# Moving the additions to the output, the gathers of output rows and one unit of the expert order

## The chip, the cores and the metric

The kernel runs on one core of a Trainium2 chip. The metric is the device time of that core in microseconds (us) from launch to end; lower is better. TensorE does the matmuls and transpositions, VectorE (DVE in the profile) and ScalarE (ACT) the element work, GpSimd (POOL) issues the indirect DMAs here (gathers and scatters by a list of row numbers), and SyncE (SP) issues the plain loads.

## The reference, cut to what matters

The reference is pooled-query attention, then a gated feed-forward layer with RMS norm, then a layer of eight experts of which each token uses two. Only the last is touched by the change:

```python
logits = x @ w_gate
noisy_logits = logits + np.log1p(np.exp(x @ w_noise)) * noise
top2 = np.argpartition(-noisy_logits, 2, axis=1)[:, :2]
...                                   # softmax over the two
out = np.zeros((N, D))                # N = 1152 tokens, D = 512
for e in range(E):                    # 8 experts
    for k in range(2):
        mask = top2[:, k] == e
        h = np.maximum(x[mask] @ w1[e], 0.0)              # 512 -> 1024
        out[mask] += top2_w[mask, k, None] * (h @ w2[e])  # 1024 -> 512
```

## The kernel before, in words

The tokens of each expert are cut into blocks of up to 128. A *unit* is one expert with two blocks (a pair) or one block (a single); unit numbers go by the list `SEQ`. Units 0 and 1 are pairs that are chosen early. Before the change units 2, 4, 6, 8, 10, 11 and 13 are pairs and units 3, 5, 7, 9 and 12 are singles. A further set of units behind a branch is for uneven routings; it does not run with these inputs.

Each unit has eight steps, `i` = 0 to 7. Steps 0 to 3 multiply the tokens by a quarter of `w1` each (`up_pair`, `up_one`; tile `ph`), steps 4 to 7 multiply the hidden values by a quarter of `w2` each and accumulate in PSUM (`down`; tile `py`). Every float32 product is made from rounded high and low parts with three passes: high by high, the low part of the tokens, the low part of the weights. ScalarE rounds the high part, and VectorE subtracts it to get the low part. The pieces around a unit are:

- `wsplit` (lines 106 and 1006): splits one quarter of weights, `raw`, into `wz`. It runs five steps ahead of its use (`LEAD = 5`), one at the end of each step, and it sets off the load of the same quarter two units later (SP, line 961).
- `gather_x` (L1022): gathers the token rows `xg`, with their weights, for the unit two ahead; one buffer.
- `x_trans` (L973, L976, L978): in step 5 TensorE transposes the next unit's tokens into a PSUM bank, ScalarE writes the high part and VectorE the low part of `xgT`. `weight` (L1120, L1122; tile `wv`) follows.
- `h_trans` (the same lines, tile `hTT`): singles alone transpose their hidden values, one half after step 2 and the other after step 4. `bank()` gives these transpositions and those of `x_trans` two PSUM banks in turn, so the second block's `x_trans` in a single takes the bank of the second `h_trans`.
- `gather_o` (L1028): gathers the rows of `out` that the unit will add to, tile `pr`, one buffer.
- `finish` (L1133, L1134): VectorE computes `yo = py * weight + pr`, and POOL scatters `yo` to `out`; for a pair there are two additions and two scatters. It is called for unit u-1 while unit u runs.

All instructions stand in the program order in which Python calls these functions, and each engine takes its own in that order. Every scatter to `out` and every gather from it waits for the scatter before it to land, since all touch the same DRAM tensor. So there is a loop through memory: the additions of a unit lead to its scatters, these to the gather of output rows of the next unit, and this to that unit's additions.

Of the kernel before, what the change touches and what calls it, by code (L numbers as in the profile page):

```python
# [21 lines left out]
def fused_kernel(ctx, tc, q, k, v, w_gate, w_val, w_out, rms_g,  # L22
# [895 lines left out]
    def r_index(pl):  # L918
# [12 lines left out]
    RAW = []  # L931
    REG = {}
    SEQ = [None, None] + [(True, 0), (False, 0), (True, 1), (False, 1), (True, 2), (False, 2), (True, 3), (False, 3),
                          (True, 4), (True, 5), (False, 4), (True, 6)]
    NU1 = len(SEQ)
    SEQ += [(True, r) for r in range(NPS, NPA)] + [(False, r) for r in range(NSS, NSA)]

    def nblk(u):
        return 2 if u < 2 or SEQ[u][0] else 1
# [48 lines left out]
    def experts():  # L988
# [5 lines left out]
        def wload(u, i):  # L994
            if i == 0:
                c = ucol(u, 0) if u > 1 else 1
                REG[u] = sp.value_load(R["ti" if u > 1 else "ea"][0:1, c:c + 1], min_val=0, max_val=NE - 1)
            e_dma(u, i)
# [9 lines left out]
        def wsplit(u, i):  # L1008
            w_hi(u, i)
            w_lo(u, i)  # L1010

        def col(u, k, nm):
            if u < 2:
                return R[nm + "0"][:, 2 * u + k:2 * u + k + 1]
            c = ucol(u, k)
            return R[nm][:, c:c + 1]

        def gather_x(u):
            XG[u] = mo.tile([P, 2, XW], F32, name="xg", tag="xg", bufs=1)
            for k in range(nblk(u)):  # L1020
                gi = col(u, k, "gidx")
                pool.indirect_dma_start(out=XG[u][:, k], out_offset=None, in_=XD if u > 1 else XD[0:QF],  # L1022
                                        in_offset=bass.IndirectOffsetOnAxis(ap=gi, axis=0))

        def gather_o(u):
            PR[u] = wps[0].tile([P, 2, DM], F32, name="pr", tag="ws21", bufs=1)
            for k in range(nblk(u)):
                pool.indirect_dma_start(out=PR[u][:, k], out_offset=None, in_=out,  # L1028
                                        in_offset=bass.IndirectOffsetOnAxis(ap=col(u, k, "gidx"), axis=0))
# [28 lines left out]
        def x_trans(u):  # L1058
            run(x_trans_(u))

        def h_trans(u, h):
            run(h_trans_(u, h))
# [30 lines left out]
        def down(u, i, k):  # L1093
            if (u, "y", k) not in PL:
                PL[u, "y", k] = pbank("py")
            w, x = W[u, i], HTT[u]
            f0 = 2 * (i - 4)
            for z, (a, c) in enumerate(PASS):
                for d in range(2):
                    pe.matmul(PL[u, "y", k], x[c][:, f0 + d, k * P:k * P + P], w[a][:, d],  # L1100
                              start=i == 4 and z + d == 0, stop=i == 7 and z == 2 and d == 1)

        def piece(u, i):
            if i >= 4:
                for k in range(nblk(u)):
                    down(u, i, k)
            elif nblk(u) == 2:
                up_pair(u, i, 0)
                up_pair(u, i, 1)
                up_evac(u, i)  # L1110
            else:
                up_one(u, i)

        def weight(u):
            n = nblk(u)
            xg = XG[u]
            wv = WV[u] = mo.tile([P, 3, 2], F32, name="wv", tag="wv", bufs=3)
            e = R["eb"][:, ucol(u, 0):ucol(u, 0) + 1] if u > 1 else R["ef"][:, u:u + 1]
            for z in range(2):
                dve.scalar_tensor_tensor(wv[:, z, 0:n], xg[:, 0:n, DM + 2 + z], e, xg[:, 0:n, DM + z],  # L1120
                                         op0=ALU.is_equal, op1=ALU.mult)
            dve.tensor_tensor(wv[:, 2, 0:n], wv[:, 0, 0:n], wv[:, 1, 0:n], op=ALU.add)  # L1122

        def finish(u, ks=None):
            if u not in YO:
                YO[u] = mo.tile([P, 2, DM], F32, name="yo", tag="yo", bufs=1)
            yo = YO[u]
            for k in range(nblk(u)) if ks is None else ks:
                w = WV[u][:, 2, k:k + 1]
                if u == 0:  # L1130
                    dve.tensor_scalar(yo[:, k], PL[u, "y", k], w, 1.0, op0=ALU.mult, op1=ALU.mult)
                else:
                    dve.scalar_tensor_tensor(yo[:, k], PL[u, "y", k], w, PR[u][:, k], op0=ALU.mult, op1=ALU.add)  # L1133
                pool.indirect_dma_start(out=out, out_offset=bass.IndirectOffsetOnAxis(ap=col(u, k, "sidx"), axis=0),  # L1134
                                        in_=yo[:, k], in_offset=None, bounds_check=B * SQ - 1, oob_is_err=False)
# [7 lines left out]
        def units(u0, u1, skip=0):  # L1143
            todo = [(u, i) for u in range(u0, u1) for i in range(8)]
            if not skip:
                gather_x(u0)
                gather_o(u0)
                for i in range(8):
                    wload(u0, i)
                for a in todo[:LEAD]:  # L1150
                    wsplit(*a)
                x_trans(u0)
                weight(u0)
                if u0 + 1 < u1:
                    gather_x(u0 + 1)
                    for i in range(8):
                        wload(u0 + 1, i)
                for u, i in todo[:LEAD]:
                    if u + 2 < u1:
                        wload(u + 2, i)  # L1160
            for n_, (u, i) in enumerate(todo):
                if n_ < skip:
                    continue
                last = u == u1 - 1
                if not last or i < 4:
                    piece(u, i)
                if nblk(u) == 1:
                    if i == 2:
                        h_trans(u, 0)
                    if i == 4 - last:  # L1170
                        h_trans(u, 1)
                if u > max(u0, 1):
                    if i == (1 if last else 3):
                        finish(u - 1)
                    if i == (1 if last else 6):
                        gather_o(u)
                if i == 5 and u + 1 < u1:
                    x_trans(u + 1)
                    weight(u + 1)
                    if u + 2 < u1:  # L1180
                        gather_x(u + 2)
                if n_ + LEAD < len(todo):
                    v_, j = todo[n_ + LEAD]
                    wsplit(v_, j)
                    if v_ + 2 < u1:
                        wload(v_ + 2, j)

            u = u1 - 1
            for k in range(nblk(u)):
                for i in range(4, 8):  # L1190
                    down(u, i, k)
                finish(u, [k])
# [4 lines left out]
        def rest():  # L1197
            open_psum()
            PL[1, "y", 0] = pbank("py")
            units(0, NU1, 8)  # L1200
            more = nc.values_load(R["more"][0:1, 0:1], min_val=0, max_val=1)  # L1201
            with tc.If(more > 0):
                units(NU1, len(SEQ))
# [53 lines left out]
    for f in range(2, NFP - 2):  # L1257
        u0 = 32 * f
        for s_, a in zip(T_E, ((f, 2), (f + 1, 0), (f + 1, 1))):
            dec(u0 + s_, *a)  # L1260
    u0 = 32 * (NFP - 2)
# [204 lines left out]
```

## Time and profile before

| what | value |
|---|---|
| median of 3 runs | 841.33 us (839.68 to 841.87) |
| the profiled execution, its own time | 845.55 us |
| span of that execution, first to last instruction | 843.3 us |
| TensorE busy | 794.3 us (94%) |
| VectorE busy | 581.2 us (69%) |
| ScalarE busy | 422.0 us (50%) |
| GpSimd busy | 303.6 us (36%) |
| mean granted TensorE clock | 0.976 of full speed |

The profiled execution took 4.2 us more than the median of the runs. TensorE's share is high everywhere; what a change in the last stage is worth has to be read from that stage, which runs from about 568 us to the end.

### The profile page before, as it was taken

Reading aid. Unit: us, or ns where it says so; the run is one execution under the profiler, and the core shown is the slowest. Engines: PE = TensorE matmul, PEld = TensorE weight load, DVE = VectorE, ACT = ScalarE, POOL = GpSimd, SP = SyncE. Lnnn points to the kernel's source line nnn. Section 1 sums busy time; section 2 is a strip of 40 time slices with the busy share of each in tenths; the row PEclk is TensorE's granted clock in tenths of the full one; section 3 lists DMA queues with packets and bytes.
Section 4 is the critical chain, followed back from the end, with each engine's and each line's share of the span. In section 5 each row is a group of like instructions: output and inputs, shape, how many; then the busy total and the mean of one; then the engine's idle time right before and its main releaser. Section 6 shows DMA issues by size and latency. Waiting matters only on the chain. (4 is left out here: it accounts for less than half of the span.)

```text
span 843.3 us, 14029 instructions
## 1 busy us (share of the span) xinstructions
PE 794.3 (94%) x5282; PEld 683.7 (81%) x5282; DVE 581.2 (69%) x838; ACT 422.0 (50%) x823; POOL 303.6 (36%) x251
## 2 busy tenths in 40 slices
PE   5999999999897979999999999999999899989994
PEld 4877777777675779998999999879989798889883
DVE  6668668677679866665687646597676677676680
ACT  4655655656665644442343252555455556554550
POOL 8647647649224531312132100113133332422331
PEclk9999999999999989999999999999999999999997
DMA  7245232221132211422142016649987879787411
GB/s 215 72 136 154 54 98 75 58 84 30 43 115 59 92 51 51 130 79 92 51 141 63 1 51 218 203 148 373 314 286 243 291 254 312 256 289 233 140 44 39
DMA packets 72939, 118.83 MB, mean 141 GB/s; under 512 B 7582, under 2 KB 37278, under 8 KB 72864
## 3 DMA queue, kind: packets, MB, share of 16 engines
q1 hardware_dynamic: 67504, 101.55, 37.8%
q0 software_dynamic: 5360, 16.31, 5.5%
q8 instruction: 43, 0.70, 0.4%
q14 instruction: 32, 0.26, 0.1%
HBM read 103.66 MB, written 10.77 MB: 136 GB/s over the span
## 5 line engine op out<-in xcount | busy, mean ns | idle before, releaser
L528 PE MATMUL gv<-XN,ws 128*128 128x256 f32 (+1 forms) x1152 | 168.1, 299 | 4.4 <-ACT sl L536 4.0
L528 PEld LDWEIGHTS gv<-XN,ws 128*128 128x128 f32 x1152 | 159.8, 191 | 10.3 <-ACT sl L536 4.2
L1006 DVE TENSOR_TENSOR wz<-raw,wz 128x1024 fp32r<-128x1024 f32 x112 | 133.8, 1222 | 22.9 <-ACT wz L106 22.3
L193 DVE TENSOR_REDUCE Ql<-s 128x1 fp32r<-128x1152 f32 x72 | 97.3, 1354 | 58.7 <-PE s L188 44.7
L1100 PE MATMUL py<-wz,hTT 128*128 128x512 f32 x552 | 137.2, 401 | 0.0
L204 ACT ACTIVATE et<-st 128x288 f32<-128x288 f32 x288 | 103.0, 413 | 52.8 <-PE st L203 48.5
L1100 PEld LDWEIGHTS py<-wz,hTT 128*128 128x128 f32 x552 | 102.9, 192 | 20.9 <-DVE hTT L978 0.7
L106 ACT CAST wz<-raw 128x1024 fp32r<-128x1024 f32 x112 | 113.4, 1046 | 8.0 <-PE py L1100 8.0
L398 POOL TENSOR_TENSOR ws<-wm,ws 128x1024 fp32r<-128x1024 f32 x18 | 43.3, 2407 | 150.7 <-ACT ws L397 96.4
L202 PE MATMUL st<-QH,KT 128*128 128x288 f32 x288 | 91.3, 332 | 5.3 <-ACT et L204 3.8
L1073 PEld LDWEIGHTS ph<-xgT,wz 128*128 128x128 f32 x768 | 92.8, 189 | 0.7
L1073 PE MATMUL ph<-xgT,wz 128*128 128x256 f32 x768 | 92.8, 281 | 0.0
L549 PE MATMUL po<-ws,hT 128*128 128x512 f32 x324 | 84.6, 400 | 0.1
L203 PE MATMUL st<-QlT,KT 128*128 128x288 f32 x288 | 82.2, 299 | 0.0
L229 PE MATMUL av<-et,v 128*64 128x288 f32 x576 | 81.9, 420 | 0.0
L1134 POOL DMA_INDIRECT out_dram<-yo,sidx x23 | 32.1, 1395 | 131.5 <-DVE yo L1133 96.0
L202 PEld LDWEIGHTS st<-QH,KT 128*128 128x128 f32 x288 | 55.0, 191 | 20.6 <-ACT et L204 11.5
L217 POOL TENSOR_TENSOR accp<-accp,et 128x576 f32<-128x576 f32 x32 | 48.6, 1519 | 55.8 <-ACT et L204 35.1
L549 PEld LDWEIGHTS po<-ws,hT 128*128 128x128 f32 x324 | 59.5, 192 | 11.1 <-ACT hT L538 0.5
L538 ACT CAST hT<-sl 128x256 fp32r<-128x256 f32 (+1 forms) x48 | 20.8, 433 | 89.8 <-DVE sl L537 89.8
L229 PEld LDWEIGHTS av<-et,v 128*64 128x64 f32 x576 | 37.6, 138 | 26.0 <-issue 5.9
L203 PEld LDWEIGHTS st<-QlT,KT 128*128 128x128 f32 x288 | 55.5, 193 | 0.0
(250 smaller groups left out, 1142.6 us busy)
## 6 DMA issues: line engine op xcount, KB each, us to landing
raw<-in_moe_w_dram SPq DMA_DIRECT2D x112, 512.0 KB, 4.6
wraw<-in_moe_w_gate_dram SPq DMA_DIRECT2D x6, 1024.0 KB, 5.5
wraw<-in_moe_w_val_dram SPq DMA_DIRECT2D x6, 1024.0 KB, 6.7
wraw<-in_moe_w_out_dram SPq DMA_DIRECT2D x6, 1024.0 KB, 5.1
kraw<-in_k_dram SPq DMA_DIRECT2D x16, 288.0 KB, 3.8
v<-in_v_dram SPq DMA_DIRECT2D x8, 576.0 KB, 3.7
KT<-KT SPq DMA_DIRECT2D x16, 288.0 KB, 3.3
Qraw<-in_q_dram SPq DMA_DIRECT2D x16, 256.0 KB, 3.9
```

Of the source, the lines that this page charges most:

```text
L106: act.copy(o, i)
L193: dve.tensor_reduce(Ql[p % 3][h][:, c, D:D + 1], t[:, :, 0:384], axis=AX.XY, op=ALU.max, negate=True)
L202: pe.matmul(t[:, 0:NG], KT[p, h][:, cs], QhT[p, h][:, n0:n0 + NG], start=True, stop=False)
L203: pe.matmul(t[:, 0:NG], KT2[h][p % NKT[h]][:, cs], QlT[p, h][:, n0:n0 + NG], start=False, stop=True)
L204: act.activation(et[:, h, :], t[:, 0:NG], AF.Exp, scale=SCALE)
L217: eng.tensor_tensor(acc, acc, e, op=ALU.add)
L229: pe.matmul(av[h * D:(h + 1) * D, 0:NG], V[p][:, h, c, :], ET[p, g, c][:, h, :], start=(c == 0), stop=(c == KC - 1))
L528: pe.matmul(t[:, 0:n], w[a][:, d, j * P:(j + 1) * P], XN[hf][b_][:, d, cs], start=(k_ == 0), stop=(k_ == 11))
L549: pe.matmul(pt, HT[f, hf][a][:, j, c0:c0 + P], w[b_][:, j, :], start=(k_ == 0), stop=(k_ == 5))
L1006: eng.tensor_tensor(lo, RAW[u % 2][i], hi.bitcast(F32), op=ALU.subtract)
L1073: pe.matmul(o, w[a][:, d, j * P:j * P + P], XT[u][c][:, d], start=z + d == 0, stop=z == 2 and d == 3)
L1100: pe.matmul(PL[u, "y", k], x[c][:, f0 + d, k * P:k * P + P], w[a][:, d], start=i == 4 and z + d == 0, stop=i == 7 and z == 2 and d == 1)
```

## The change

It does three things. `finish(u - 1)` is called in a pair at step 4 instead of step 3, and in a single at step 5 instead of step 3; the call now stands behind `x_trans`, `weight` and `gather_x` of the same step. `gather_o(u)` is called in a pair at step 5 instead of step 6, and in a single at step 7 instead of step 6. The last unit keeps step 1 for both. And the fifth single changes places with the sixth pair behind it in the list: units 10 to 13 are now pair, single, pair, pair.

```diff
     SEQ = [None, None] + [(True, 0), (False, 0), (True, 1), (False, 1), (True, 2), (False, 2), (True, 3), (False, 3),
-                          (True, 4), (True, 5), (False, 4), (True, 6)]
+                          (True, 4), (False, 4), (True, 5), (True, 6)]
...
-                if u > max(u0, 1):
-                    if i == (1 if last else 3):
-                        finish(u - 1)
-                    if i == (1 if last else 6):
-                        gather_o(u)
                 if i == 5 and u + 1 < u1:
                     x_trans(u + 1)
                     weight(u + 1)
                     if u + 2 < u1:
                         gather_x(u + 2)
+
+                f_, g_ = (1, 1) if last else (4, 5) if nblk(u) == 2 else (5, 7)
+                if u > max(u0, 1):
+                    if i == f_:
+                        finish(u - 1)
+                    if i == g_:
+                        gather_o(u)
                 if n_ + LEAD < len(todo):
```

On VectorE the first place is a single, from the low part of its first hidden half to the first weights behind the next unit's tokens. Before:

```order
L978 TENSOR_TENSOR hTT<-xt,hTT 128x4x128
L1006 TENSOR_TENSOR wz<-raw_5871,wz 128x1024
L1133 SCALAR_TENSOR_TENSOR yo<-py,wv,pr 128x512 x2
L1006 TENSOR_TENSOR wz<-raw_5581,wz 128x1024
L978 TENSOR_TENSOR hTT<-xt,hTT 128x4x128
L1006 TENSOR_TENSOR wz<-raw_5581,wz 128x1024
L978 TENSOR_TENSOR xgT<-xt,xgT 128x4x128 x2
L1120 SCALAR_TENSOR_TENSOR wv<-xg,eb 128x2 x2
L1122 TENSOR_TENSOR wv<-wv 128x2
L1006 TENSOR_TENSOR wz<-raw_5582,wz 128x1024 x2
```

With the change the same stretch of a single on VectorE reads:

```order
L978 TENSOR_TENSOR hTT<-xt,hTT 128x4x128
L1006 TENSOR_TENSOR wz<-raw_5871,wz 128x1024
L1006 TENSOR_TENSOR wz<-raw_5581,wz 128x1024
L978 TENSOR_TENSOR hTT<-xt,hTT 128x4x128
L1006 TENSOR_TENSOR wz<-raw_5581,wz 128x1024
L978 TENSOR_TENSOR xgT<-xt,xgT 128x4x128 x2
L1120 SCALAR_TENSOR_TENSOR wv<-xg,eb 128x2 x2
L1122 TENSOR_TENSOR wv<-wv 128x2
L1133 SCALAR_TENSOR_TENSOR yo<-py,wv,pr 128x512 x2
L1006 TENSOR_TENSOR wz<-raw_5582,wz 128x1024 x2
```

The two additions `yo` of the pair before have moved from ahead of the second `hTT` to behind the next unit's `xgT` and `wv`.

The second place is POOL's queue over a single and the pair behind it, from the gather of token rows or the scatters of the single's steps to the pair's gather of output rows. Before:

```order
L1134 DMA out_dram<-yo,sidx 1152x512 x2
L1022 DMA xg<-XD,gidx 128x516
L1028 DMA pr<-out_dram,gidx 128x512
L1134 DMA out_dram<-yo,sidx 1152x512
L1022 DMA xg<-XD,gidx 128x516 x2
L1028 DMA pr<-out_dram,gidx 128x512 x2
```

With the change POOL takes the same stretch in this order:

```order
L1022 DMA xg<-XD,gidx 128x516
L1134 DMA out_dram<-yo,sidx 1152x512 x2
L1028 DMA pr<-out_dram,gidx 128x512
L1134 DMA out_dram<-yo,sidx 1152x512
L1022 DMA xg<-XD,gidx 128x516 x2
L1028 DMA pr<-out_dram,gidx 128x512 x2
```

In the single the gather of token rows now stands ahead of the two scatters; the order within the pair is the same, although its calls stand at other steps.

## Rows read from the trace of the kernel before

**Rows 1.** Waits in the expert stage: waiter <- releaser: us in total, times, longest.

```profile
PE xt L973 <- DVE hTT L978: 10.5, 5, 3.6
```

**Rows 2.** Timeline of unit 5, second half: start, duration, work [idle before <-releaser].

```profile
662.35 0.75 DVE L1133 SCALAR_TENSOR_TENSOR yo<-py,wv,pr 128x512 f32<-128x512 f32 x1 [2.21 <-DMA pr<-out_dram,gidx]
...
665.99 0.69 PE L973 MATMUL xt<-ident,xg 128*128 128x128 f32 x4 [3.59 <-DVE hTT L978]
666.40 4.58 PE L1100 MATMUL py<-wz,hTT 128*128 128x512 f32 x12
...
670.82 11.56 PE L1073 MATMUL ph<-xgT,wz 128*128 128x256 f32 x96
```

**Rows 3.** Timeline around the end of unit 12, TensorE and VectorE.

```profile
805.43 0.66 PE L973 MATMUL xt<-ident,xg 128*128 128x128 f32 x4 [0.85 <-DVE hTT L978]
805.84 3.00 PE L1100 MATMUL py<-wz,hTT 128*128 128x512 f32 x12
...
808.00 0.16 DVE L1122 TENSOR_TENSOR wv<-wv 128x2 f32<-128x2 f32 x1
808.68 11.69 PE L1073 MATMUL ph<-xgT,wz 128*128 128x256 f32 x96
```

**Rows 4.** Stretches of 20 us: PE, PEld, DVE, ACT, POOL busy, granted clock, DMA share, GB/s.

```profile
640.00:660.00 20.00, 20.00 (x122) 17.61 (x121) 13.42 (x16) 11.14 (x14) 7.80 (x6) 1.00 0.71 235
660.00:680.00 20.00, 16.41 (x109) 14.93 (x108) 13.40 (x18) 9.36 (x13) 4.92 (x4) 0.91 0.89 297
```

**Rows 5.** Timeline from unit 3's scatters through unit 4 into unit 5.

```profile
624.68 2.00 POOL L1134 DMA_INDIRECT out_dram<-yo,sidx  x1 [5.94 <-DVE yo L1133]
...
629.71 11.56 PE L1073 MATMUL ph<-xgT,wz 128*128 128x256 f32 x96
...
632.87 1.00 POOL L1134 DMA_INDIRECT out_dram<-yo,sidx  x1 [6.18 <-DVE wz L1006]
...
639.82 0.96 POOL L1028 DMA_INDIRECT pr<-out_dram,gidx  x1 [4.66 <-DMA out_dram<-yo,sidx]
...
646.25 0.75 DVE L1133 SCALAR_TENSOR_TENSOR yo<-py,wv,pr 128x512 f32<-128x512 f32 x1 [3.62 <-DMA pr<-out_dram,gidx]
...
652.48 4.39 PE L1088 MATMUL ph<-wz,xgT 128*128 128x256 f32 x36
...
657.07 1.22 DVE L1006 TENSOR_TENSOR wz<-raw,wz 128x1024 fp32r<-128x1024 f32 x1 [2.20 <-ACT wz L106]
```

**Rows 6.** Timeline: first scatters in units 5 and 7, additions in units 6 and 8.

```profile
664.28 1.96 POOL L1134 DMA_INDIRECT out_dram<-yo,sidx  x1 [7.22 <-DVE yo L1133]
...
683.66 0.74 DVE L1133 SCALAR_TENSOR_TENSOR yo<-py,wv,pr 128x512 f32<-128x512 f32 x1
...
703.47 1.97 POOL L1134 DMA_INDIRECT out_dram<-yo,sidx  x1 [5.75 <-DVE yo L1133]
...
723.52 0.75 DVE L1133 SCALAR_TENSOR_TENSOR yo<-py,wv,pr 128x512 f32<-128x512 f32 x1 [2.15 <-DMA pr<-out_dram,gidx]
```

**Rows 7.** Timeline of POOL in units 12 and 13.

```profile
803.26 1.02 POOL L1134 DMA_INDIRECT out_dram<-yo,sidx  x1 [4.58 <-DVE yo L1133]
...
806.84 1.00 POOL L1134 DMA_INDIRECT out_dram<-yo,sidx  x1 [2.56 <-DVE wz L1006]
...
809.90 1.75 POOL L1028 DMA_INDIRECT pr<-out_dram,gidx  x1 [2.06 <-DMA out_dram<-yo,sidx]
```

**Rows 8.** The tile `pr`, its gathers, all of the execution.

```profile
DMA to landing us min/median/max: 4.7/5.8/9.2
```

**Rows 9.** Timeline of unit 13: the additions on VectorE and the last scatter.

```profile
815.88 0.74 DVE L1133 SCALAR_TENSOR_TENSOR yo<-py,wv,pr 128x512 f32<-128x512 f32 x1
...
825.88 0.75 DVE L1133 SCALAR_TENSOR_TENSOR yo<-py,wv,pr 128x512 f32<-128x512 f32 x1 [4.16 <-PE py L1100]
...
832.35 1.00 POOL L1134 DMA_INDIRECT out_dram<-yo,sidx  x1 [4.42 <-DVE yo L1133]
```

**Rows 10.** Waits of VectorE in the expert stage, as in rows 1.

```profile
DVE yo L1133 <- DMA pr<-out_dram,gidx: 11.4, 9, 3.6
```

## The prediction

> **What bounds the kernel now.** I read the waits of the expert stage first, then the timeline of the singles, then the gathers and scatters. TensorE is busy nearly without a break in the pairs; its one wait of size stands in the five singles. There it has the transposition of the second token block to do, and the bank for it is freed by VectorE's low part of the second hidden half: 10.5 us in five waits [rows 1]. The timeline of unit 5 shows why VectorE is late. Two additions stand ahead of that low part, and the first waits 2.21 us for its gathered output rows; TensorE starts at 665.99, after 3.59 us idle [rows 2]. In unit 12 the output rows are there in time, the additions cost their two times 0.75 us, and the wait is 0.85 us [rows 3].
>
> The idle time has a second price. After it the twelve matmuls of the next two steps took 4.58 us in unit 5 [rows 2] against 3.00 in unit 12 [rows 3], and the granted clock of that stretch is 0.91 where the one before had 1.00 [rows 4]. Unit 9 repeats this; the other three singles, with shorter waits, do not.
>
> Behind this stands a loop through memory. The single scatters its pair's sums, one scatter after the other, then the single's own output rows are gathered, and the next pair adds to them. From the first scatter to that addition it took 646.25 - 624.68 = 21.6 us [rows 5] and 723.52 - 703.47 = 20.1 [rows 6], where the addition was waiting. At the other two it was not waiting, so that the chain took at most 683.66 - 664.28 = 19.4 [rows 6]; I use 19.0.
>
> **The change, part by part.**
>
> *The wait of TensorE goes.* In a single the additions now stand behind the low parts and the weights of the next tokens. Ahead of the second hidden half only splits are left, which ScalarE feeds. In unit 12 the two additions are 1.5 us of work for a wait of 0.85 [rows 3], so taking them out leaves nothing there; in the other four the wait for output rows leaves too. This removes 10.5 us [rows 1], and the slow matmuls twice, 2 x (4.58 - 3.00) = 3.2 [rows 2, 3]. I leave 0.1 per single, 0.5 in all (bounds: 0, and unit 12's 0.85 each, 4.3), for the last split to finish. Net gain 13.2 us.
>
> *The addition in the pair becomes later than VectorE wants it.* Call the pair's first matmul p. In unit 12 the weights of the next tokens were done at 808.16, 0.5 us before p = 808.68 [rows 3]. TensorE's bank and VectorE's later instructions both follow from the second hidden half, so this distance should hold. POOL then issues the gather of token rows of that step, which now stands ahead of the scatters; with an issue of 1.0 us, as those of the scatters [rows 7], and a start on either side of it, an estimate of 0.5 each, the first scatter follows at about p + 1.5. It can't be before p + 0.3, when the first sum is ready, and two issues of 2.0 us as that of 624.68 [rows 5] would make it p + 2.5. Before, it was 5.0 us ahead of p in unit 3 (624.68 against 629.71 [rows 5]) and 6.5 in unit 5 [rows 2, 6]. The chain then ends at p + 23.1, 20.5, 21.6 and 20.5 for the four pairs behind a single with weights still being loaded. VectorE comes to the addition at 683.66 - 670.82 = 12.8 after p [rows 2, 6] and, one step later, behind one split more of 1.2, at p + 14.1. So it will stand for 6 to 9 us at each of these, against 3.6 in unit 4.
>
> What is queued behind it: one split, the low part of the single's tokens, its weights, and the splits for the single. ScalarE and TensorE go on, since the pair's own weights were split five steps ahead. In unit 4 VectorE came out of its wait at 646.25 - 629.71 = p + 16.5, and in the single behind it still had 2.20 us of idle time at 657.07, just ahead of the first hidden half that TensorE waits for [rows 5]. The change leaves one split (1.2) less between. So TensorE loses nothing up to p + 16.5 + 2.2 + 1.2 = p + 19.9, and from there on microsecond for microsecond. The loss is 3.2 + 0.6 + 1.7 + 0.6 = 6.1 us. It is cut into two waits, at the single's start and at its hidden half, so that it is less likely to bring the clock down: I take half of one 1.6 us, 0.8 (bounds 0 and 3.2).
>
> The bounds of this term: nothing if all four chains are like the short ones and the scatter starts at p + 0.3 (19.7), and 4 x 3.2 = 12.8 if all are like that of unit 3.
>
> A rule of the Trainium skill bears on the hops of the chain ("DMA: Bandwidth & Descriptors", section "Anatomy of one DMA — SWDGE (gpsimd) path"): about 2.0 us fixed plus the bytes over 436 GB/s. For a block of 262 KB it would give 2.6 us a hop, and with three issues of 1 us a chain of about 11 us and no new wait at all. While weights are loaded this case's hops took 8.2 and 6.9 us from scatter to scatter and from scatter to gather [rows 5]; without loads 3.6 and 3.1 [rows 7], which is near the page. The sum goes by the rows.
>
> *The pair's gather of output rows one step earlier* is hidden: POOL takes it behind the two gathers of token rows as before, and these wait for VectorE's weights, so an earlier call is worth nothing. The single's gather one step later waits for the second scatter anyway; it too changes nothing. The gather of token rows that now goes ahead is not needed before the next unit's step 5.
>
> *The order of units.* The number of units and matmuls stays. The weights of the last unit are loaded by the third step of unit 11, which is now the single, so the chain that starts there runs without loads: 3.6 + 3.1 [rows 7] + at least 4.7 [rows 8], with p + 1.5 it ends near p + 13, before VectorE asks. No wait there. But the last unit now finishes a pair: two scatters, the second behind the first. Its additions ran 815.88 - 808.68 = 7.2 after its start [rows 3, 9]; 1.0 to the scatter, 3.6 to the second, 3.1 to the gather of output rows, 5.0 until they are added: 19.9, against 825.88 - 808.68 = 17.2 when TensorE had the first block ready [rows 9]. The first of the last two scatters comes at 20.9, the second 3.6 behind at 24.5, against 832.35 - 808.68 = 23.7 [rows 9]. That is 0.8 later, 1.9 if the gather lands in its median 5.8 [rows 8]. I take 1.0.
>
> **The sum.** -13.2 + 6.1 + 0.8 + 1.0 = -5.3 us. The profiled execution's own 845.55 becomes 840.2; it stands 4.2 above the median of the runs, 841.33, which becomes 836.0. A measurement of this kernel can tell about 0.3% from no change, 2.5 us: faster is below 838.8, slower above 843.9.
>
> **Rivals.**
>
> *The chain is hidden (0.17).* If the hops are shorter while VectorE stands still and sets off no weight loads, the chain ends by p + 19.9 everywhere. For it: two of four were at most 19.4. Against it: the other two. Time: -13.2 + 1.0 = -12.2, 829.1. The skill's rule on the hops, above, would end here.
>
> *The gain is eaten (0.17).* The loop through memory sets the pace of a pair and a single, wherever the additions stand. For it: unit 3's chain of 21.6, and VectorE waiting for output rows already, 11.4 us in all [rows 10]. If all four chains took that long: -13.2 + 12.8 + 0.8 + 1.0 = +1.4, 842.7.
>
> *Slower: the wait at the pair's addition grows (0.12).* Place: the addition in the pair's step 4. A gather of output rows took up to 9.2 us to land [rows 8], against 6.4 in unit 3's chain (639.82 to 646.25 [rows 5]). Two such chains of 24.4 end at p + 25.9 and cost 6.0 each; two of 21.6 cost 3.2 each; TensorE then waits long enough in one piece for the slow matmuls twice: 18.4 + 3.2 + 1.0 - 13.2 = +9.4, 850.7. It decides from a mean end of the chain of about p + 23.5, where four losses of 3.6 plus 0.8 and 1.0 exceed the gain by 2.5.
>
> **How the numbers follow.** My forecast has 0.54: a gain of 2.6 to 11 us, most likely 5.3. With the hidden chain that makes faster 0.71; same 0.17; slower 0.12. The range reaches from the hidden chain, 829, to the eaten gain with one more microsecond, 843.5; I leave about 0.2 outside, more of it above.
>
> **What would show it right or wrong.** The wait of TensorE for the second hidden half should fall from 10.5 us to under 1, and the matmuls behind it should take 2.9 to 3.0 us. VectorE's wait for output rows should rise from 11.4 [rows 10] to between 25 and 35 us, nearly all in four additions at 20 to 23 us after their pair's start. TensorE should show new waits for `xgT` or the first `hTT` in the singles behind them, 6 us in all. The last scatter should start about 24.5 us after the last unit. It is wrong if the pair's additions wait little (time near 829), or if token rows, whose gather stands behind VectorE's wait in the pair, reach the next single's step 5 too late. I cost that at nothing: behind the addition VectorE has one split, one low part and the weights, some 3 us, before these gathers can go, and the single's second transposition could start 665.99 - 3.59 - 652.48 = 9.9 us into it [rows 2, 5], about 12 after the addition; a landing later than that costs TensorE as much as it is late, four times.

## The result and the profile after

The changed kernel took 833.14 us in the median of its runs against 841.33 before: a ratio of 0.9902, with a 95% interval of 0.9877 to 0.9927, 8.2 us faster. That lies inside the range, and the forecast of 836.0 named the right side, but the gain is half as large again as the 5.3 us that were forecast. The profiled execution took 833.25 us (span 831.1), which is near its median; that of before, at 845.55, stood 4.2 above its own. So the two profiles differ by 12.3 us and the medians by 8.2, and what follows counts in the profiles first.

The waits of the expert stage after the change (waiter <- releaser: us in total, times, longest); the last is all that TensorE's matmuls wait for in the stage:

```profile
DVE yo L1133 <- DMA pr<-out_dram,gidx: 26.1, 7, 5.8
...
PE xt L973 <- DMA xg<-XD,gidx: 0.5, 1, 0.5
```

TensorE's 10.5 us behind `hTT` [rows 1] are gone. The other row is the time that VectorE stands idle for output rows (its *stand*, below), which rose from 11.4 us [rows 10] to 26.1: the wait was not removed, it was moved to VectorE, as the prediction said. Of the 26.1 us 18.8 lie in the four pairs that the prediction meant, 4.3 to 5.4 each, and 5.8 in the last unit.

Unit 5, the pair behind it and the last two units in the timeline (start, duration, work, in brackets the idle time before and what ended it):

```profile
658.35 1.08 PE L973 MATMUL xt<-ident,xg 128*128 128x128 f32 x8
...
659.19 3.02 PE L1100 MATMUL py<-wz,hTT 128*128 128x512 f32 x12
...
661.54 1.41 DVE L1133 SCALAR_TENSOR_TENSOR yo<-py,wv,pr 128x512 f32<-128x512 f32 x2
662.05 11.56 PE L1073 MATMUL ph<-xgT,wz 128*128 128x256 f32 x96
663.44 1.53 POOL L1134 DMA_INDIRECT out_dram<-yo,sidx  x1 [0.30 <-issue]
...
670.93 1.00 POOL L1134 DMA_INDIRECT out_dram<-yo,sidx  x1 [5.96 <-DVE wz L1006]
...
676.72 0.99 POOL L1028 DMA_INDIRECT pr<-out_dram,gidx  x1 [4.80 <-DMA out_dram<-yo,sidx]
...
681.80 0.75 DVE L1133 SCALAR_TENSOR_TENSOR yo<-py,wv,pr 128x512 f32<-128x512 f32 x1 [5.37 <-DMA pr<-out_dram,gidx]
...
684.82 4.39 PE L1088 MATMUL ph<-wz,xgT 128*128 128x256 f32 x36
...
793.56 11.69 PE L1073 MATMUL ph<-xgT,wz 128*128 128x256 f32 x96
...
800.76 1.40 DVE L1133 SCALAR_TENSOR_TENSOR yo<-py,wv,pr 128x512 f32<-128x512 f32 x2
801.78 1.02 POOL L1134 DMA_INDIRECT out_dram<-yo,sidx  x1 [7.32 <-DVE yo L1133]
...
810.19 0.96 POOL L1028 DMA_INDIRECT pr<-out_dram,gidx  x1 [0.30 <-issue]
...
812.45 0.75 DVE L1133 SCALAR_TENSOR_TENSOR yo<-py,wv,pr 128x512 f32<-128x512 f32 x1 [5.84 <-DMA pr<-out_dram,gidx]
...
815.00 1.02 POOL L1134 DMA_INDIRECT out_dram<-yo,sidx  x1 [3.85 <-DMA pr<-out_dram,gidx]
...
816.21 0.75 DVE L1133 SCALAR_TENSOR_TENSOR yo<-py,wv,pr 128x512 f32<-128x512 f32 x1 [3.01 <-PE py L1100]
820.37 1.00 POOL L1134 DMA_INDIRECT out_dram<-yo,sidx  x1 [4.34 <-DMA out_dram<-yo,sidx]
```

*The single* (the first three kinds of row). The transpositions of both token blocks now run as one group of eight without a wait at 658.35, the twelve matmuls behind them took 3.02 us where unit 5 took 4.58 [rows 2], and the two additions stand behind the work that TensorE needs. Taken over the five singles, from the first `ph` matmul to the next pair's first, TensorE needed 79.6 us before and 66.0 after. These 13.6 us are the 10.5 of waits, the 3.2 of slow matmuls and 0.8 for the group of eight that the wait had cut in two (0.84 us from its start to the matmuls behind it, where the two halves had needed 1.01 beside the wait), less 0.9 in two singles that are longer than the others after the change. Of this 0.5 is a wait for token rows, and the rest comes with a weight load that waits 0.35 us for the second half of `hTT`.

*The pair.* Counted from its first matmul p = 662.05, the first scatter starts at p + 1.4 and the addition at p + 19.75. The other three chains end at p + 18.8, 19.2 and 18.7. VectorE stands 5.4 us ahead of this addition, and TensorE starts the next single at 684.82 without a wait.

*The end.* From the last unit's first matmul to the start of the last scatter it is 820.37 - 793.56 = 26.8 us, against 23.7 before [rows 3, 9]. The first block's sum is ready at 813.2 but its scatter starts at 815.00: it waits for the second block's gather from `out`, issued at 810.19, to land. The last scatter then waits for the first to land, though its sum is ready at 816.96. That is 3.1 us longer, where 1.0 was forecast.

So the changed part is 13.6 - 3.1 = 10.5 us shorter in the profiles. Unit 1's first matmul comes 1.4 us earlier after the change, in work that the diff does not touch, and some tenths lie outside the spans.

### The profile page after: what moved, and what is told of

It is laid out like the page before. It is cut to its first block, busy times and chain, and to the rows that moved or that the text cites. A ratio compares the mean times of both kernels' runs of the same rounds, so it can differ in the third digit from the quotient of the medians.

```text
span 831.1 us, 14029 instructions
## 1 busy us (share of the span) xinstructions
PE 788.2 (95%) x5282; PEld 678.8 (82%) x5282; DVE 578.8 (70%) x838; ACT 421.3 (51%) x823; POOL 304.1 (37%) x251
## 4 chain that ended last, share of the span: by engine, by line
PE 72%; DVE 10%; issue 5%; ACT 4%; POOL 4%; DMA 3%; another core or an unknown queue 1%; POOLq 0%; DVEq 0%; ACTq 0%
PE gv L528 14%; PE py L1100 13%; PE ph L1073 11%; PE po L549 7%; PE av L229 7%; PE st L202 4%; PE s L188 3%; PE st L203 3%; PE tt L135 2%; PE ph L1088 2%; DMA xg<-XD,gidx 2%; DVE Ql L193 1%; PE xt L973 1%; DVE es L217 1%; ACT et L204 1%
## 5 line engine op out<-in xcount | busy, mean ns | idle before, releaser
L1006 DVE TENSOR_TENSOR wz<-raw,wz 128x1024 fp32r<-128x1024 f32 x112 | 134.1, 1222 | 14.2 <-ACT wz L106 10.5
L1100 PE MATMUL py<-wz,hTT 128*128 128x512 f32 x552 | 134.1, 394 | 0.0
L1100 PEld LDWEIGHTS py<-wz,hTT 128*128 128x128 f32 x552 | 100.7, 188 | 20.2 <-DVE hTT L978 0.6
L549 PEld LDWEIGHTS po<-ws,hT 128*128 128x128 f32 x324 | 58.4, 188 | 10.7 <-ACT hT L538 0.5
```

The lines of the kernel that those rows point to most:

```text
L549: pe.matmul(pt, HT[f, hf][a][:, j, c0:c0 + P], w[b_][:, j, :], start=(k_ == 0), stop=(k_ == 5))
L1006: eng.tensor_tensor(lo, RAW[u % 2][i], hi.bitcast(F32), op=ALU.subtract)
```

## The experiments

Ratios are to the kernel before on the same chip, with the 95% interval.

**1. How far the profiled execution of before is typical.** The kernel before, unchanged, looked at again.

> The kernel before, unchanged, once more: its profiled execution took 845.55 us, 4.2 more than the median of its runs. Theory (that execution was slow by chance, in the waits of TensorE in the singles): a second profile stands nearer to 841 us and shows less than 10.5 us of waits for the second hidden half, or fewer slow matmuls behind them. Rival (the profile itself adds 4 us to this kernel): 845 to 846 us again, with the same 10 to 11 us.

It took 840.36 us. Two of its singles in the timeline:

```profile
624.31 0.66 PE L973 MATMUL xt<-ident,xg 128*128 128x128 f32 x4 [1.97 <-DVE hTT L978]
624.73 4.58 PE L1100 MATMUL py<-wz,hTT 128*128 128x512 f32 x12
...
664.16 0.65 PE L973 MATMUL xt<-ident,xg 128*128 128x128 f32 x4 [2.35 <-DVE hTT L978]
664.57 3.00 PE L1100 MATMUL py<-wz,hTT 128*128 128x512 f32 x12
```

The waits summed to 9.2 us, none over 2.4, and one single of the five had slow matmuls. Waits and slow matmuls cost 10.8 us here against 13.7 in the first profile: 2.9 of the 5.2 us between the two executions. What the change can win differs from one execution to the next, and the sum against the first profile started from an expensive one. Another 2.2 us lie ahead of unit 1, whose first matmul starts at 566.29 here and at 568.47 in the first profile, in work that the diff does not touch. Against this execution the singles are 10.7 us shorter after the change and the end 3.1 longer: 7.6 us in all, near the 8.2 of the medians.

**2. The steps alone, and the order of units alone.** `steps_only` is the changed kernel with the old list; `seq_only` is the kernel before with the new one. The diff is that of `steps_only`, `seq_only` has its reverse in the kernel before:

```diff
-                          (True, 4), (False, 4), (True, 5), (True, 6)]
+                          (True, 4), (True, 5), (False, 4), (True, 6)]
```

> The changed steps with the old order of units (pair, pair, single, pair at the end). Theory: the new steps carry the whole gain, and the new order only keeps the last single's chain away from the last unit. In the old order that chain starts at about 1.5 us after the last unit's start and ends 11 to 12 us later, at about 13, where VectorE wants it at 7.2; so VectorE stands 6 us there, TensorE loses 1 to 2 us in the last unit and the last scatter starts some 28 us after the unit's start against 26.8 in the changed kernel: 1 to 3 us slower than the changed kernel, 834 to 836 us. Rival (the order of units is worth nothing): within 1 us of the changed kernel, and the last scatter at 26 to 27.

> The old steps with the new order of units. Theory: the waits of TensorE for the second hidden half stay, 10 us or more in five singles, since the order of units does nothing for them, the fifth single now stands where weights are loaded and waits 1.5 to 3.5 us in place of 0.85, and the last unit finishes a pair, 3 us later at the end: 843 to 847 us, 0.2 to 0.7% slower than the kernel before. Rival (the new order carries a good part of the gain): 838 us or less.

`steps_only` took 833.46 us, 0.9895 (0.9878 to 0.9913): as the full change, so the theory of 834 to 836 us fell. Its last single does set off a chain into the last unit, in the timeline:

```profile
792.30 7.97 PE L1073 MATMUL ph<-xgT,wz 128*128 128x256 f32 x65
...
803.54 0.75 DVE L1133 SCALAR_TENSOR_TENSOR yo<-py,wv,pr 128x512 f32<-128x512 f32 x1 [3.96 <-DMA pr<-out_dram,gidx]
...
817.58 1.00 POOL L1134 DMA_INDIRECT out_dram<-yo,sidx  x1 [2.77 <-DMA out_dram<-yo,sidx]
```

The addition that VectorE waits for stands 11.2 us after the unit's start, VectorE loses 3.96 us and TensorE none; the last scatter starts 25.3 after the last unit. `seq_only` took 846.02 us, 1.0039 (1.0020 to 1.0057), 3.3 us slower, and its waits read:

```profile
PE xt L973 <- DVE hTT L978: 11.3, 5, 2.8
```

With the old steps the wait stays whatever the list is, and the fifth single, now with loads beside it, waits 2.60 us where unit 12 waited 0.85 [rows 3]. So the new list costs time with the old steps, and with the new ones it wins nothing that can be seen beside the two measurements of the full change, 0.9902 and 0.9859 (experiment 6).

**3. The singles' steps alone, and the pairs' alone.** Both with the new list; `single_only` as shown, `pair_only` with `(4, 5)` for pairs and `(3, 6)` for singles.

```diff
-                f_, g_ = (1, 1) if last else (4, 5) if nblk(u) == 2 else (5, 7)
+                f_, g_ = (1, 1) if last else (3, 6) if nblk(u) == 2 else (5, 7)
```

> The changed kernel, but pairs keep their old steps (addition at step 3, gather of output rows at step 6); singles have the new ones, and the order of units is new. Theory: the gain comes from the singles, where TensorE's 10.5 us of waits stood. In the pair VectorE now stands one step earlier with two splits behind it in place of one, so that TensorE loses nothing up to about 18.7 us after the pair's start; the chain ends at 17.4 to 19.8 us: 0 to 4 us slower than the changed kernel, 833 to 837 us. Rival (pair and single each carry half): 836 to 839 us and waits of TensorE in the singles of 4 us or more.

> The changed kernel, but singles keep their old steps (additions at step 3, gather at step 6); pairs have the new ones, and the order of units is new. Theory: TensorE's waits for the second hidden half stay at 10 us or more, since the additions still stand ahead of it in the singles; 842 to 847 us, no faster than the kernel before. Rival (the pair's earlier gather or later addition shortens the loop, so that output rows come in time for the single's step 3): waits of 4 us at most and 836 us or less.

`single_only` took 834.05 us, 0.9914 (0.9896 to 0.9932); `pair_only` 846.65 us, 1.0069 (1.0051 to 1.0087), and its waits still hold

```profile
PE xt L973 <- DVE hTT L978: 11.7, 5, 2.5
```

The gain is the singles' move. With the pair's addition left a step earlier VectorE stands 30.7 us instead of 26.1 and TensorE waits some 3 us, none of it put down to `hTT`. In the profiles its singles take 2.8 us longer than after the change, but its end is 2.0 us shorter (experiment 4). The median lies within the interval of the first measurement of the full change, so what the pairs' move adds is not clear.

**4. The last unit's calls one step earlier.** `last0`, and the same kernel again as `last0_again` on another chip:

```diff
-                f_, g_ = (1, 1) if last else (4, 5) if nblk(u) == 2 else (5, 7)
+                f_, g_ = (0, 0) if last else (4, 5) if nblk(u) == 2 else (5, 7)
```

> The changed kernel with the additions and the gather of output rows of the last unit at step 0 in place of step 1. Theory: in the changed kernel the end is set by the chain additions, two scatters, two gathers, addition, scatter, scatter, which starts 7.2 us after the last unit's start and ends 26.8 after it, 3.1 later than in the kernel before, where TensorE set the end. One step earlier moves the whole chain by 2.85 us: last scatter at 24 to 24.5 us, 2.3 to 2.9 us faster than the changed kernel. Rival (the end is set by TensorE's last matmuls, or VectorE standing at the earlier addition holds TensorE): less than 1 us of gain.

> The changed kernel with the last unit's additions and gather at step 0, once more, since the changed kernel came out at 0.9902 and 0.9859 of the kernel before in two jobs and this version at 0.9867 in one. Theory (the end of the changed kernel stands 1.5 to 3 us behind TensorE's last matmuls, and step 0 takes that away): 0.983 to 0.986, the last scatter within 24 us of the last unit's start. Rival (the two are the same within what runs of this kernel scatter): 0.986 to 0.990.

831.53 and 830.92 us, 0.9867 (0.9848 to 0.9886) and 0.9872 (0.9851 to 0.9893). The end of `last0_again` in the timeline:

```profile
794.08 11.69 PE L1073 MATMUL ph<-xgT,wz 128*128 128x256 f32 x96
...
798.40 1.40 DVE L1133 SCALAR_TENSOR_TENSOR yo<-py,wv,pr 128x512 f32<-128x512 f32 x2
...
816.72 0.75 DVE L1133 SCALAR_TENSOR_TENSOR yo<-py,wv,pr 128x512 f32<-128x512 f32 x1 [4.69 <-PE py L1100]
817.75 1.00 POOL L1134 DMA_INDIRECT out_dram<-yo,sidx  x1 [4.42 <-DVE yo L1133]
```

The additions run 4.3 us after the last unit's start instead of 7.2, and the last scatter waits for its own sum, which waits for TensorE: 23.7 us in all, 3.1 less than after the change. But the 26.8 us after the change are not fixed. `single_only` has the same last unit and ends so:

```profile
796.90 11.69 PE L1073 MATMUL ph<-xgT,wz 128*128 128x256 f32 x96
...
821.73 1.00 POOL L1134 DMA_INDIRECT out_dram<-yo,sidx  x1 [2.82 <-DMA out_dram<-yo,sidx]
```

That is 24.8 us; `pair_only` and `seq_only` show 25.0, `after_again` and `twice` 26.6. In all of them the first of the last two scatters starts 21.0 to 21.4 us after the unit; the difference is the hop (the time from one DMA's start to the start of what waits for it) from there to the last, 3.8 to 3.9 us or 5.2 to 5.4, and no run shows what decides it. So `last0` wins 1.1 to 3.1 us at the end, and the medians don't settle it, since the changed kernel came out at 0.9902 in one measurement and at 0.9859 in another (`after_again`, below).

**5. The chain made longer.** `twice` gathers a single's output rows twice, the second gather behind the first, so that the pair's addition comes later and it shows from which point on TensorE loses time (its threshold).

```diff
-            for k in range(nblk(u)):
+            for k in list(range(nblk(u))) * (2 if nblk(u) == 1 else 1):
```

> The changed kernel, but a single's output rows are gathered twice into the same tile, the second gather behind the first, so that the loop through memory is 5 to 6.5 us longer at each single; the result is the same. In the changed kernel the pair's addition began 18.8, 19.8, 19.2 and 18.7 us after the pair's start in the four loaded pairs, and TensorE lost nothing. Theory (TensorE loses nothing up to p + 19.9 and each microsecond beyond): the addition comes at 24 to 26 us, TensorE loses 4 to 6 us at each of the four, in waits for the low part of the next tokens and of the first hidden half; 849 to 857 us. Rival one (the loss begins later, since VectorE has more slack than counted): less than 2 us a pair, 842 us or less. Rival two (the loop through memory sets the pace already in the changed kernel): the whole 5 to 6.5 us at each of five singles, 858 to 866 us.

It took 847.82 us, 1.0079 (1.0058 to 1.0100), just under the 849 to 857 of the theory and well above the 842 of its first rival. Three of its four cases in the timeline, pair's start, addition, and the next single's first matmuls:

```profile
626.72 11.56 PE L1073 MATMUL ph<-xgT,wz 128*128 128x256 f32 x96
...
640.79 1.18 POOL L1028 DMA_INDIRECT pr<-out_dram,gidx  x1 [4.51 <-DMA out_dram<-yo,sidx]
...
646.20 0.97 POOL L1028 DMA_INDIRECT pr<-out_dram,gidx  x1 [4.24 <-DMA pr<-out_dram,gidx]
...
649.71 0.75 DVE L1133 SCALAR_TENSOR_TENSOR yo<-py,wv,pr 128x512 f32<-128x512 f32 x1 [8.61 <-DMA pr<-out_dram,gidx]
...
652.25 5.56 PE L1088 MATMUL ph<-wz,xgT 128*128 128x256 f32 x32 [2.12 <-DVE xgT L978]
...
693.96 5.57 PE L1088 MATMUL ph<-wz,xgT 128*128 128x256 f32 x32 [3.92 <-DVE xgT L978]
...
708.14 11.56 PE L1073 MATMUL ph<-xgT,wz 128*128 128x256 f32 x96
...
730.42 0.75 DVE L1133 SCALAR_TENSOR_TENSOR yo<-py,wv,pr 128x512 f32<-128x512 f32 x1 [7.89 <-DMA pr<-out_dram,gidx]
732.95 4.06 PE L1088 MATMUL ph<-wz,xgT 128*128 128x256 f32 x32 [1.40 <-DVE xgT L978]
...
739.69 1.19 PE L1100 MATMUL py<-wz,hTT 128*128 128x512 f32 x4 [0.35 <-DVE hTT L978]
```

The first addition stands at 649.71 - 626.72 = p + 22.99 and TensorE waits 2.12 us; the last one shown at p + 22.28 and it waits 1.40. The other two stand at p + 24.8 and p + 22.5, with waits of 3.92 and 1.67. All four give a threshold of p + 20.9 for the first wait, after which TensorE pays microsecond for microsecond. A second wait of 0.35 for the first half of `hTT` makes it p + 20.5 for both together. After the waits of 2.12 and 3.92 us the next 32 matmuls took 5.56 and 5.57 us instead of 4.06, and the granted clock of one stretch behind the first is 0.50 (stretch, then PE, PEld, DVE, ACT and POOL busy, clock, DMA share, GB/s):

```profile
654.00:656.00 2.00, 2.00 (x11) 2.00 (x11) 2.00 (x3) 0.34 (x1) 1.70 (x2) 0.50 0.84 282
```

The chain does price a pair as the prediction argued; in the first profile of the changed kernel it only ends too early to do so. Other executions with these steps reach the threshold: in `last0` one such addition is

```profile
684.72 0.75 DVE L1133 SCALAR_TENSOR_TENSOR yo<-py,wv,pr 128x512 f32<-128x512 f32 x1 [6.66 <-DMA pr<-out_dram,gidx]
```

which is 21.0 us after its pair's start at 663.68. TensorE waits 0.16 and 0.38 us behind it, which gives p + 20.5 again, without the second gather.

**6. The weight loads taken away.** `noload_b` is the kernel before and `noload_a` the changed one, with

```diff
+            if u >= 4:
+                return
```

ahead of the loads of a quarter.

> The kernel before with the expert weights of units 4 to 13 not loaded (the splits take what units 2 and 3 left in the buffers, so the values of these units are those of the wrong experts); all other work is the same. It tells the two parts of TensorE's 9 to 11 us of waits in the singles apart. Theory (the longer part is the wait for output rows, which the loads lengthen: hops of 6 to 8 us with loads, 3.1 to 3.6 without): the additions no longer wait, each single's wait falls to the 0.85 us of unit 12, 4 to 4.5 us in all, no slow matmuls: 6 to 9 us faster than the kernel before, 833 to 836 us. Rival (the additions' own place is the matter, not the rows): the waits stay at 9 us or more and the time within 2 us of the kernel before.

> The changed kernel with the expert weights of units 4 to 13 not loaded, as in the run beside it (wrong experts' values in these units, the same work). Theory (what the loads lengthen is hidden in the changed kernel, up to a wait for token rows of half a microsecond): VectorE's wait for output rows falls from 26 us to under 3, and the time by no more than 2 us against the changed kernel. Rival (the loads still cost the changed kernel time, in the chain or in the matmuls): 4 us faster or more.

> The changed kernel, unchanged, beside the others for comparison. 832 to 834.5 us; waits of TensorE in the singles of no more than 1.5 us, all for token rows; the last scatter 25 to 27 us after the last unit's start.

`noload_b` took 834.51 us, 0.9903 (0.9887 to 0.9918), and its waits hold

```profile
PE xt L973 <- DVE hTT L978: 4.3, 5, 0.9
```

All five waits are of unit 12's size: 4.3 us are the two additions' own place ahead of the low part, the rest of the 9 to 11 us is the wait for output rows, and that exists only beside loads. `noload_a` took 830.93 us, 0.9867 (0.9847 to 0.9888), and `after_again` beside it 831.65, 0.9859 (0.9844 to 0.9875): once the additions stand behind, the loads cost nothing that the times show. The waits of `noload_a` (two more lines in the file, so L1133 reads L1135) and its first chain in the timeline:

```profile
DVE yo L1135 <- DMA pr<-out_dram,gidx: 6.4, 2, 5.5
```

```profile
625.84 1.58 POOL L1136 DMA_INDIRECT out_dram<-yo,sidx  x1 [0.30 <-issue]
...
629.97 1.44 POOL L1136 DMA_INDIRECT out_dram<-yo,sidx  x1 [2.55 <-DVE hTT L1080]
...
633.47 0.99 POOL L1030 DMA_INDIRECT pr<-out_dram,gidx  x1 [2.06 <-DMA out_dram<-yo,sidx]
```

From scatter to scatter it is 4.1 us and from scatter to gather 3.5 (4.1 to 4.4 and 2.8 to 3.5 over its four chains), where the same hops in unit 6 after the change took 7.5 and 5.8. VectorE's one long wait, 5.5 us, is that of the last unit, which the expectation had forgotten.

**7. The pair's stand moved on.** In `pair5` (with `last0`'s edit) the pair's addition stands one step later, behind the work for the next unit's tokens, so that VectorE should not stand:

```diff
-                f_, g_ = (1, 1) if last else (4, 5) if nblk(u) == 2 else (5, 7)
+                f_, g_ = (0, 0) if last else (5, 5) if nblk(u) == 2 else (5, 7)
```

> The changed kernel with the last unit's additions at step 0 and, in pairs, the addition at step 5 behind the next tokens' transposition, weights and gather, as in singles. VectorE then wants the addition at about 19 us after the pair's start in place of 14, the low part of the single's tokens no longer stands behind it, and the gather of token rows goes ahead of it. Theory (the slack is what counts): the losses of 0.2 to 0.9 us for token rows and for the low part at some singles go, 0 to 2 us faster than the run with step 0 in the last unit alone, 828.5 to 831.5 us; the stand of VectorE falls under 10 us in all. Rival (VectorE's stand is what quiets the DMA queues and keeps the chain short; without it the hops grow back to 20 us and the next single's additions come late): 2 us slower or more, with waits of TensorE for hidden halves or of VectorE in the singles.

It took 856.11 us, 1.0149 (1.0127 to 1.0171), the slowest of all, where the theory had 828.5 to 831.5. Its waits, and the addition in a pair with the single behind it, up to the next pair:

```profile
PE ph L1073 <- DVE hTT L1078: 19.2, 5, 7.0
```

```profile
655.20 0.75 DVE L1133 SCALAR_TENSOR_TENSOR yo<-py,wv,pr 128x512 f32<-128x512 f32 x1
...
659.37 1.03 POOL L1134 DMA_INDIRECT out_dram<-yo,sidx  x1 [0.30 <-issue]
...
667.57 1.13 POOL L1028 DMA_INDIRECT pr<-out_dram,gidx  x1 [7.18 <-DMA out_dram<-yo,sidx]
...
676.59 0.75 DVE L1133 SCALAR_TENSOR_TENSOR yo<-py,wv,pr 128x512 f32<-128x512 f32 x1 [2.38 <-DMA pr<-out_dram,gidx]
...
681.40 7.48 PE L1073 MATMUL ph<-xgT,wz 128*128 128x256 f32 x48 [3.76 <-DVE hTT L1078]
```

The pair adds later, so the next scatter, the gather behind it (667.57) and the single's additions (676.59, after a wait) come later too. VectorE then reaches the next pair's first low part late, and TensorE stands 3.76 us. The wait for memory had been harmless where VectorE stood in the pair; one unit on, it is not. Whether the hops grow without the stand, as the rival had it, this run does not tell apart: VectorE comes to the pair's addition after its rows in every pair, so the trace shows no end of the chain there.

## Why the prediction was right and where it was wrong

**The wait of TensorE: right.** TensorE's matmuls no longer wait for `hTT`, where they had waited 10.5 us, the slow matmuls went with it, and the singles gave back 13.6 us against 13.2 forecast. `single_only` and `pair_only` show that this is the singles' move alone.

**The loss at the pair's addition: wrong in both of its numbers.** The step that failed is "The chain then ends at p + 23.1, 20.5, 21.6 and 20.5" with "TensorE loses nothing up to ... p + 19.9". Measured, the chains end at p + 18.8, 19.75, 19.2 and 18.7, and `twice` puts the threshold at p + 20.5. So 6.1 + 0.8 us became nothing; the 0.9 us in two singles is neither of the two waits that were forecast, and VectorE stood 4.3 to 5.4 us at each addition instead of 6 to 9. The scatter's start at p + 1.0 to 1.4 was as forecast (p + 1.5); it is the length that was over-estimated, 17.4 to 18.4 us instead of 19.0 to 21.6. One profile flatters this a little: in `after_again` one chain took 19.1 us and TensorE waited 0.3 behind it, in `last0` one took 20.0 and it waited 0.5.

Why the chains are shorter is shown only in part. The 21.6 us of unit 3 was a long case: in `b_again` the three chains at which the addition waited took 18.4, 19.9 and 19.5. Then there is VectorE's stand at the end of the chain, in which its splits don't run, and the loads that they set off don't start. Stretches of the changed kernel in the pair at p = 662.05, where the stand begins at 676.4 (columns as in experiment 5):

```profile
672.00:676.00 4.00, 4.00 (x26) 3.54 (x25) 2.83 (x4) 2.69 (x4) 0.00 (x0) 1.00 0.98 335
676.00:680.00 4.00, 4.00 (x21) 3.37 (x20) 0.43 (x1) 0.57 (x2) 0.99 (x1) 1.00 0.81 265
680.00:682.00 2.00, 2.00 (x10) 1.63 (x10) 0.20 (x1) 2.00 (x4) 0.00 (x0) 1.00 0.12 46
```

Ahead of the stand the DMA share is 0.98; by its end it is 0.12. The hops of this chain were 7.5, 5.8 and 5.1 us, the last one, which lies in the stand, the shortest. In `twice` it is plainer: the second of two gathers, late in the stand, took 3.5 us (646.20 to 649.71) beside 5.4 for the first. That loads lengthen hops is shown by taking them away; that the stand shortens its own last hop is read from these windows and `twice`, not isolated by a run of its own. And it is not the whole cause: VectorE had stood 3.6 us at the end of unit 4's chain too, whose last hop took 6.4 us [rows 5], and the middle hop, which is over about when the stand begins, was 5.2 to 6.2 us in the four pairs against 6.9 in unit 4, with the DMA share still at 0.98. Why that hop is shorter stays open.

This is the rival of the hidden chain, with 0.17, by its result. Its chance was too low, because the two chains of at most 19.4 us and the two of 20 to 22, all from one execution, were taken as equal evidence. The rule on the hops in the Trainium skill ("DMA: Bandwidth & Descriptors", "Anatomy of one DMA — SWDGE (gpsimd) path") points to the same end, but not by its size: an estimate from it was 2.6 us a hop, and the traces show 2.8 to 4.4 without loads (`noload_a`; 3.1 and 3.6 in [rows 7]) and 5.2 to 8.6 beside loads, ahead of the stand (the chains after the change and [rows 5]).

**The end: too low in this profile.** The term of +1.0 measured +3.1. It missed that a scatter to `out` also waits for gathers from `out` issued ahead of it (815.00 instead of about 813.5); since the sum was ready earlier than forecast, this put the first of the last two scatters only 0.5 us later, at 21.4 instead of 20.9. The rest is the last hop, 5.4 us instead of 3.6. In the three runs of experiment 4 in which that hop took 3.8 to 3.9 us the end came out 1.2 to 1.3 us longer than before, near the forecast.

**The order of units: priced at the end only.** The prediction counted it as a chain without loads in the last pair and +1.0. That chain did not end near p + 13 but at p + 15.6, after 1.2 us of VectorE's stand, and cost TensorE nothing. Against the old order the new one shows no gain with the new steps (0.9895 beside 0.9902 and 0.9859) and costs 3 us with the old.

**The sum.** By measured terms it is -13.6 + 3.1 = -10.5 us in the profiles. Against the medians it is -8.2, because the profiled execution of before lost 2.9 us more to waits and slow matmuls than `b_again` did (experiment 1); against `b_again` it comes to -7.6. That 836.0 stood within 3 us of 833.14 is in part luck: 6.9 us of loss that did not come stand against 2.1 too little at the end and the 2.9 that the first profile had over the second. What splits the runs of the kernel before, 838.4 to 844.3 us over all measurements, stays open beyond these 2.9 and the 2.2 ahead of unit 1.

**The token rows**, named as what could go wrong, do come late, by little: 0.5 and 0.9 us in all in the two profiles of the changed kernel, and at most 2.1 in the other kernels with the new steps in the singles.

## What to carry to other kernels

A wait for memory costs by what stands behind it on the waiting engine, not by its length: 19 us of VectorE's stand in the pairs cost TensorE nothing, while before the change 5.6 us of it in the singles, with the additions behind it, held TensorE up for 10.5 us and cost nearly 14. Before moving such a wait, count the slack of the place (here some 20.5 us from the pair's start) and measure it by making the chain longer on purpose; a step further on, TensorE waited 19 us elsewhere. And don't carry the length of a chain of transfers, taken from a few cases of one execution, to another place in the program: here it came out some 2 us shorter, and that decided whether the pairs cost anything.

## What the hardware showed beside this

TensorE's clock falls behind some of its waits only. Waits of 1.97 us (experiment 1) and of 2.12 us (`twice`) were followed by slow matmuls, twelve in 4.58 us and 32 in 5.56, the latter at a granted clock of 0.50, the lower of its two levels (1.2 and 2.4 GHz); behind a wait of 2.35 us in the same execution as the first, twelve took 3.00. Each drop cost 1.5 to 1.6 us. So the price of a wait of about 2 us is uncertain by nearly its own length, and that is part of the scatter between runs of one kernel.
